# A's blocks 55 steps apart, a block's first scores ahead, and block sums copied by VectorE in a two-attention kernel

## The chip, the cores and the metric

The kernel runs on one core of a Trainium2 chip. The metric is the device time of one execution in microseconds (us); "the time" of a kernel is the median of its timed runs. A profile is one more execution, with its own time.

## The reference, cut to what matters

Two attentions over 2048 positions of width 576 with 32 heads of 18 are computed in fp32, and their outputs stand side by side. A looks, for each position, at 8 positions behind it at distances 0, 2, ..., 14. B looks at all 2048.

```python
def _A_ref(x, wqkv, wo):          # H = 32; Dh = 18; W, dil = 8, 2
    q, k, v = ...                 # x @ wqkv, split into heads
    idx = pos[:, None] - jnp.arange(W) * dil
    logits = jnp.einsum("bhsd,bhswd->bhsw", q, kg) * scale
    logits = jnp.where(idx >= 0, logits, -1e9)
    o = jnp.einsum("bhsw,bhswd->bhsd", _softmax(logits), vg)
    return concat_heads(o) @ wo

def _B_ref(x, wqkv, wo):
    scores = jnp.einsum("bhqd,bhkd->bhqk", q, k) * scale
    o = jnp.einsum("bhqk,bhkd->bhqd", _softmax(scores), v)
    return concat_heads(o) @ wo

return jnp.concatenate([a, b], axis=-1)
```

## The kernel before

Everything is one instruction stream per engine in an order written out by hand (`manual_schedule`). Each engine does its instructions in the order in which the program emits them; so do the queues, of which SP's carries nearly all transfers. An instruction waits where it stands, and everything behind it on its engine or queue waits with it. The waits themselves are put in by the framework: for data, for a buffer that is still read, and for a transfer that has to land.

**Stages.** First come the projections (lines 304 to 717). With them run the first maxima of B. Then comes the main loop (lines 1139 to 1180) of 512 steps, of which step 0 is emitted with the projections. At its end lie B's last output products and `closing`.

**A step.** Step s works on block n = s // 16 of B and on key tile kt = s % 16. A block is one group g = n // 4 of four heads and one stretch b = n % 4 of 512 queries. In a step TensorE forms the scores of four heads (`score`, line 256, matmul at line 263), 128 keys by 512 queries each, into a ring of four PSUM banks. ScalarE takes each exponential out of its bank (line 268). The step's products with the values are emitted one step later by `weigh` (line 728, matmul at line 731) and add up over the block's 16 steps in the bank `po`. There is one `po`. After the last key tile, in the step with kt = 0 of the next block, `finish` (line 736) copies `po` into the tile `o` by ScalarE (line 740) and plans the division and the store over the next 26 steps.

**Maxima.** The exponent of a query needs its row maximum beforehand. Therefore TensorE also forms the scores with queries and keys exchanged (`take`, line 160), and VectorE reduces each bank to its maxima (`reduce`, line 168). These run ahead of the scores by some blocks. A step has three such reductions: `maximum(1)`, the half pieces of both row groups (`parts_of_maximum`, line 233, shared by two steps) and `maximum(0)`. Their matmuls use a ring of three banks. In the order of TensorE a step is: one half piece, score 0, `maximum(1)`, score 2, score 1, the other half piece, score 3, `maximum(0)`, then the eight instructions of line 731. When 64 reductions of a block are there, `least` (line 173) takes the block's negated maximum, `turn` transposes it one step later, `halve` (on GpSimd, lines 103 and 104) splits it one step after that, and `place` (line 191) writes it with eight small SP transfers into rows 54, 55 and 118, 119 of the block's query tile `qs`. From halve to place are 5 steps, or 2 in the last group. A block's first score waits for its eight transfers.

**Agenda.** `plan(start, pieces)` and `later(n, f)` put functions into `agenda[step]`. `due()` runs those of the current step at its end. `inside` holds functions that the next step runs ahead of its last score.

**A.** A's attention is done in 8 blocks of 256 positions by GpSimd, spread over the main loop by `local(j)` (line 845). The pieces of block j stand at fixed distances from its start, which is 10 + 54 j: nine `match` (lines 868 and 872) at distance 5 to 25, VectorE's maxima over the window (`most`, line 886) at 31 to 33, `lower` (line 892) at 33, the exponential at 35, the sums (`total`) at 36 to 38, `share` (line 905) at 39, nine `weighted` (lines 911 to 914) at 39 to 59, `upper` and `rest` at 60 and 61, and two stores to DRAM (`put`) at 64 and 66. `get` loads the result back transposed (six SP transfers, lines 936 and 938) into the tiles `at0`, `at1` and `ahl`, of which there is one each. Two products with the output weights follow for each of the two halves of 128 positions (`sums_of_a`, line 946, matmuls at line 1036), in the steps after those that `MADE` lists. The second half's `get` stands at the step in which the first half's second product runs. So it waits on SP until TensorE has done with the tiles. A product carries two maxima with it while there are any. `producing` is the set of steps that have a product of A or B in them.

**The last group.** `fetch_old(b)` (line 980) loads B's finished head outputs back, eight SP transfers each of 126 rows of 2 KB. They stand at steps 448 + 4, 24, 34 and 36 for b = 0, 1, 3 and 2. `full` and `partial` plan B's output products (`sum_of`, line 1044): VectorE copies one bank (line 1055) and adds the other (line 1056).

Of the kernel before, what the change touches and what calls it, by code (L numbers as in the profile page):

```python
# [10 lines left out]
AF = mybir.ActivationFunctionType  # L11
# [8 lines left out]
DH = 18  # L20
# [19 lines left out]
EARLY_PAIRS = EARLY * NB * PIECES + 2  # L40
AHEAD = 7

GAP = 54

A_FROM = 10

MADE = ((88, 96, 112, 128), (144, 160, 176, 192), (201, 208, 224, 240), (250, 256, 272, 288),
        (304, 320, 336, 352), (361, 368, 384, 400), (412, 416, 432, 448), (466, 468, 475, 480))


def ap(t, *dims):
# [10 lines left out]
def two_attentions(ctx: ExitStack, tc, xa, wa, woa, xb, wb, wob, out):  # L62
# [190 lines left out]
    e_room = None  # L253
    counted = [-1]

    def score(g, b, kt, h, kind="scores"):

        assert (g, b) in placed
        qs, ks = sets[g % 3]
        p, r = divmod(h, 2)  # L260
        ps = bank(kind)
        at = slice(64 * r, 64 * r + 56)
        nc.tensor.matmul(ps, ks[at, p, 128 * kt : 128 * kt + 128], qs[at, b, p], start=True, stop=True)  # L263

        counted[0] += 1
        early = counted[0] % 8 < 6
        e = (e_room if early else work).tile([128, 512], F32, name="e", bufs=6 if early else 2)
        nc.scalar.activation(e, ps, AF.Exp, scale=SCALE)  # L268
        return e
# [466 lines left out]
    def finish(g, b):  # L736
        o = work.tile([128, 512], F32, name="o", bufs=2)
        if g == NG - 1 and b == NB - 1:
            return closing(b, o, work.tile([128, 512], F32, name="rec", bufs=1))
        nc.scalar.activation(o, po, AF.Copy)  # L740
        den = work.tile([128, 16], F32, name="den", bufs=2)
        rec = work.tile([128, 512], F32, name="rec", bufs=1)
        parts = []

        def room():
            if g == NG - 1 and b == 0:

                parts[:] = [ap(work.tile([128, 4, 128], F32R, name=f"at{i}", bufs=1), (1, 512)) for i in range(2)]
            else:
                n = work.tile([128, 2, 512], F32R, name="n", bufs=1)  # L750
                parts[:] = n[:, 0], n[:, 1], n
            return parts

        if g == NG - 1 and b > 0:
            return shortly(b, o, rec, *room()[:2])

        def store():
            if g < NG - 1:
                load(do[:, g, :, 512 * b : 512 * b + 512].rearrange("i p n -> p i n"), parts[2].bitcast(F32))
            else:  # L760
                plan(step, full(b, parts))

        for at, f in ((1, lambda: load(den, o[DH:128:32])),
                      (8, lambda: nc.vector.reciprocal(den, den)),
                      (9, lambda: load(drec[g, b].rearrange("i (p n) -> (i p) n", n=16), den)),
                      (13, lambda: load(rec, rows(drec[g, b], (512, 4), (0, 32), (1, 512)))),
                      (18, lambda: nc.gpsimd.tensor_mul(o, o, rec)),  # L767
                      (19, lambda: nc.gpsimd.tensor_copy(room()[0], o)),
                      (20, lambda: nc.gpsimd.tensor_sub(parts[1], o, parts[0])),
                      (26, store)):  # L770
            later(at, f)
# [47 lines left out]
    wo = {}  # L819

    producing = set()

    def load_wo(k, src, *pieces):

# [20 lines left out]
    def local(j):  # L845
# [20 lines left out]
        def match(c):  # L866
            pr = wide()
            nc.gpsimd.tensor_mul(pr, ap(st["q"][:, 2 * c], (SUB, 2), (0, W), (1, SUB)), window(st["k"], c))  # L868
            if c == 0:
                st["pr"] = pr  # L870
            else:
                nc.gpsimd.tensor_add(st["pr"], st["pr"], pr)  # L872
            if c == DH // 2 - 1:
                lg = st["lg"] = work.tile([128, W, SUB], F32, name="lg", bufs=1)
                nc.gpsimd.tensor_add(lg, st["pr"][:, 0], st["pr"][:, 1])
                if j == 0:
                    for w in range(1, W):
                        nc.gpsimd.memset(lg[:32, w, : DIL * w], MASKED)
# [46 lines left out]
        def put(i):  # L925
            load(rows(dao[j, i, 0, 0], (DH * SUB, 128), (1, DH * SUB)),
                 ap(st["parts"][i].bitcast(F32), (1, DH * SUB)))
# [18 lines left out]
        def sums_of_a(h):  # L946
# [7 lines left out]
            nc.scalar.activation(y, two, AF.Copy)  # L954
            behind_scores.append(lambda: nc.vector.tensor_add(y, one, y))

        pieces = [(33, lower), (35, exponents), (39, share), (60, upper), (61, rest), (64, lambda: put(0)), (66, lambda: put(1))]

        pieces[:0] = [(at, lambda f=f, n=n: f(n)) for f, ats in ((most, (31, 32, 33)), (total, (36, 37, 38)),
                                                                (inverses, (38, 39))) for n, at in enumerate(ats)]  # L960
        for c in range(DH // 2):
            pieces.append((5 + 5 * c // 2, lambda c=c: match(c)))
            pieces.append((39 + 5 * c // 2, lambda c=c: weighted(c)))

        for nm, at, apart in (("q", -18, 2), ("k", -10, 2)) if j else (("q", -9, 1), ("k", -5, 1)):
            pieces += [(at + apart * i, lambda nm=nm, i=i: fetch(nm, i)) for i in range(4)]
        pieces += [(16 + 2 * i, lambda i=i: fetch("v", i)) for i in range(4)]
        made = [p - A_FROM - GAP * j for p in MADE[j]]
        for n, ends in enumerate((made[:2], made[2:])):
            pieces.append((max(ends[0] - 8, made[1] + 1 if n else 0), lambda n=n: get(n)))  # L970
            for h in range(2):
                pieces.append((ends[h], lambda h=h: finished(h)))
                producing.add(A_FROM + GAP * j + ends[h] + 1)
            pieces.append((ends[1] + 6, lambda n=n: load(out[p0 + 128 * n : p0 + 128 * n + 128, :D], ys["a", j, n])))
        return pieces

# [67 lines left out]
    def sum_of(y, t, h, chunks, kind=None):  # L1044

        pos, cols = slice(128 * t, 128 * t + 128), slice(288 * h, 288 * h + 288)
        both = []
        for r in range(2):
            both.append([])
            for c, (hi, lo) in enumerate(chunks):  # L1050
                at = slice(64 * r, min(64 * r + 64, hi.shape[0]))
                whi, wlo = wo["b"][c]
                both[r] += [(a[at, pos], w[at, cols]) for a, w in ((hi, whi), (hi, wlo), (lo, whi))]
        one, two = beside(kind, *both)
        nc.vector.tensor_copy(y, one)
        nc.vector.tensor_add(y, two, y)

    def first(t, b, h):
# [55 lines left out]
    ):  # L1114
        plan(start, [(4 * c, lambda k=k, src=src, ch=ch: load_wo(k, src, *ch)) for c, ch in enumerate(chunks)])
    for j in range(NJ):
        plan(A_FROM + GAP * j, local(j))
    for g in range(1, NG):
        if g > EARLY:
            plan(STEPS * (g - 2) + 1, [(n, f) for n, f in enumerate(stack_loads(g))])  # L1120
        if g == NG - 1:
            plan(STEPS * g, [(4, lambda: fetch_old(0)), (24, lambda: fetch_old(1)), (34, lambda: fetch_old(3)),
                             (36, lambda: fetch_old(2))])
            plan(STEPS * g, [(n, lambda t=t, h=h: partial(t, h)) for n, (t, h) in
                             zip((40, 41, 42, 44, 46, 48), [(t, h) for t in range(3) for h in range(2)])])
            plan(STEPS * g, [(62, lambda: outside.append(lambda: first(3, NB - 1, 0)))])
            for b in range(NB - 1):
                producing.update(STEPS * g + NT * (b + 1) + (31 if b == 0 else 7) + n for n in range(8))
        plan(STEPS * (g - 1), [(24, lambda g=g: load_v(g))])
# [10 lines left out]
    while step < ALL:  # L1140
        n, kt = divmod(step, NT)
        g, b = divmod(n, NB)
        es = [None] * 4

        whole = total - sum(given) > 1
        parts = bool(begun) or total - sum(given) > 3

        ps = bank() if inside and whole else None
        if parts:
            part = parts_of_maximum()  # L1150
        for h in (0, 2, 1, 3):

            if inside and h == 3:
                inside.pop(0)()
            es[h] = score(g, b, kt, h)
            if h == 0 and whole:
                maximum(1, ps)()
            if h == 1 and parts:
                part()
            if h == 3 and whole:  # L1160
                maximum(0)()
        for fs in (behind_scores, outside):
            while fs:
                fs.pop(0)()

        paired = paired or kt % 2 == 0 and sum(given) == total and not begun
        for _ in range(1 if paired and step < ALL - 2 else len(waiting)):
            if waiting:
                waiting.pop(0)()
        if ready and (kt % 2 == 0 or not paired):  # L1170
            weigh(ready.pop(0))
        ready.append((g, b, kt, es))
        if paired and kt % 2:
            weigh(*ready)
            ready.clear()
        due()

        if len(waiting) > (0 if not paired else 2 if kt % 2 else len(waiting)):
            waiting.pop(0)()
        step += 1  # L1180
# [24 lines left out]
```

## Time and profile before

| what | value |
|---|---|
| timed runs | 1616.1, 1617.08, 1619.99 us; median 1617.08 |
| the profiled execution's own time | 1616.82 us |
| its span, first to last instruction | 1615.0 us |
| projections, to the first exponential of the main loop | 413.8 us |
| main loop to step 480 | 1067.8 us |
| steps 480 to 511 | 120.4 us |
| the rest | 13.0 us |

In the page, a group's row gives line, engine, operation, output and inputs with shapes, count, then busy time, mean ns of one, idle time of the engine just before, and what ended it. A row of the timeline gives the start from the span's beginning, the duration, engine, line, operation and count; in square brackets is the idle time of the engine just before it and what ended that. PEld is TensorE's weight load, which runs ahead of and beside PE's matmuls. SPq is the issuing of transfers on SP's queue; a row gives the time of issue and not of landing. A row of the waits gives who waited for whom, the total in us, the count and the longest. The view of windows gives, for each stretch, its length and then each engine's busy time with its count of instructions, the granted TensorE clock as a share, the DMA engines' busy share and GB/s. Since each step ends with the eight matmuls of line 731, their starts are used as marks of the steps.

### The profile page before, as it was taken

What the parts mean: (1) busy time and instruction counts of PE and PEld (TensorE: products, weight loads), DVE (VectorE), ACT (ScalarE), POOL (GpSimd) and SP (SyncE); (2) the same over time, 40 slices, a digit from 0 to 9 for tenths busy, and PEclk for the clock granted to TensorE, in tenths of its full rate; (3) what the DMA queues carried; (4) which work ended last, traced back from release to release, by engine and by line L of the source; (5) the groups of instructions that cost most, each with busy time, mean ns of one, the idle gap of its engine ahead of it and who ended that gap; (6) DMA issues with size and microseconds to landing.
All of it is one profiled execution on the core that took longest, in us unless ns stands there. A gap on an engine that the chain in (4) does not pass through costs nothing.

```text
span 1615.0 us, 35230 instructions
## 1 busy us (share of the span) xinstructions
PE 1599.0 (99%) x13394; PEld 959.5 (59%) x13394; DVE 1393.9 (86%) x2366; ACT 1212.4 (75%) x2419; POOL 961.1 (60%) x792
## 2 busy tenths in 40 slices
PE   9999999999999999999999999999999999999998
PEld 7999888999544444444444444444444444445676
DVE  5199999999899998999999999999999999999532
ACT  6424442121799998999999999999999999998444
POOL 2405742210265995996995995995996997920000
PEclk9999999999999999999999999999999999999999
DMA  8937954432222262254235235332532241034201
GB/s 250 239 121 196 275 164 133 134 104 79 60 56 64 73 147 54 62 118 113 62 85 133 72 98 115 98 91 60 125 106 58 59 135 47 22 124 139 89 38 60
DMA packets 186058, 172.11 MB, mean 107 GB/s; under 512 B 119152, under 2 KB 132976, under 8 KB 184160
## 3 DMA queue, kind: packets, MB, share of 16 engines
q1 hardware_dynamic: 181024, 158.31, 35.3%
q0 software_dynamic: 4032, 10.63, 3.1%
q8 instruction: 105, 1.72, 0.5%
q10 hardware_dynamic: 832, 0.92, 0.2%
q14 instruction: 65, 0.53, 0.1%
HBM read 96.94 MB, written 71.90 MB: 105 GB/s over the span
## 4 chain that ended last, share of the span: by engine, by line
PE 82%; POOL 7%; DVE 5%; DMA 3%; ACT 2%; issue 1%; SPq 0%; POOLq 0%; DVEq 0%; ACTq 0%
PE po L731 24%; PE bank L160 15%; PE bank L353 15%; PE bank L263 15%; PE bank L1036 8%; PE bank L290 5%; DVE mx L168 4%; ACT e L268 2%; POOL pr L868 1%; POOL pr L872 1%; POOL pr L911 1%; DMA akv<-da 1%; DMA dqk<-olo 1%; POOL pr L912 1%; POOL pr L913 0%
## 5 line engine op out<-in xcount | busy, mean ns | idle before, releaser
L168 DVE TENSOR_REDUCE mx<-bank 128x2 f32<-128x512 f32 x2048 | 1286.0, 684 | 114.5 <-PE bank L160 86.2
L268 ACT ACTIVATE e<-bank 128x512 f32<-128x512 f32 x2048 | 1050.2, 607 | 90.3 <-PE bank L263 83.2
L160 PE MATMUL bank<-ks,qs 54*128 54x256 f32 (+1 forms) x2536 | 791.8, 377 | 7.4 <-DVE mx L168 5.9
L160 PEld LDWEIGHTS bank<-ks,qs 54*128 54x128 f32 x2536 | 411.3, 184 | 464.6 <-DVE mx L168 423.4
L263 PE MATMUL bank<-qs,ks 56*128 56x512 f32 x2048 | 567.3, 426 | 0.1
L731 PE MATMUL po<-e,v 128*19 128x512 f32 x4096 | 537.9, 599 | 0.0
L263 PEld LDWEIGHTS bank<-qs,ks 56*128 56x128 f32 x2048 | 299.3, 185 | 14.7 <-issue 7.5
L868 POOL TENSOR_TENSOR pr<-aq,akv 128x1024 f32<-128x1024 f32 x72 | 158.5, 2202 | 15.4 <-DMA akv<-da 12.8
L911 POOL TENSOR_TENSOR pr<-lg,akv 128x1024 f32<-128x1024 f32 x72 | 158.5, 2201 | 0.6
L872 POOL TENSOR_TENSOR pr<-pr 128x1024 f32<-128x1024 f32 x64 | 152.6, 2384 | 5.0
L731 PEld LDWEIGHTS po<-e,v 128*19 128x19 f32 x4096 | 70.5, 97 | 129.4 <-issue 127.0
L681 ACT ACTIVATE ohi<-bank 128x512 f32<-128x512 f32 (+1 forms) x56 | 30.4, 595 | 152.5 <-issue 100.7
L353 PE MATMUL bank<-xhi,ahi 64*128 64x512 f32 (+1 forms) x448 | 113.5, 387 | 0.0
L353 PE MATMUL bank<-xhi,alo 64*128 64x512 f32 (+1 forms) x448 | 112.3, 387 | 0.0
L353 PE MATMUL bank<-xlo,ahi 64*128 64x512 f32 (+1 forms) x448 | 111.9, 388 | 0.1
L912 POOL TENSOR_TENSOR pr<-pr 128x512 f32<-128x512 f32 x72 | 92.5, 1285 | 5.6
L401 POOL TENSOR_TENSOR alo<-raw,ahi 128x512 fp32r<-128x512 f32 (+1 forms) x14 | 17.6, 1258 | 120.7 <-ACT ahi L400 88.8
L493 POOL TENSOR_TENSOR olo<-olo,ohi 128x512 fp32r<-128x512 f32 x36 | 46.2, 1294 | 66.1 <-ACT ohi L492 57.5
L767 POOL TENSOR_TENSOR o<-o,rec 128x512 f32<-128x512 f32 x29 | 37.6, 1297 | 58.7 <-ACT e L268 34.2
L103 POOL CAST mh<-mt 128x32 fp32r<-128x32 f32 x32 | 6.9, 217 | 102.3 <-DVE mt L183 99.5
L353 PEld LDWEIGHTS bank<-xhi,ahi 64*128 64x128 f32 (+1 forms) x448 | 65.0, 181 | 2.9
L353 PEld LDWEIGHTS bank<-xhi,alo 64*128 64x128 f32 (+1 forms) x448 | 63.9, 182 | 2.9
(197 smaller groups left out, 1827.6 us busy)
## 6 DMA issues: line engine op xcount, KB each, us to landing
do<-n SPq DMA_DIRECT2D x28, 512.0 KB
da<-ohi SPq DMA_DIRECT2D x52, 256.0 KB
akv<-da SPq DMA_DIRECT2D x64, 175.5 KB
out<-y SPq DMA_DIRECT2D x32, 288.0 KB
qs<-dqk SPq DMA_DIRECT2D x30, 288.0 KB
ks<-dqk SPq DMA_DIRECT2D x30, 288.0 KB
at<-dao SPq DMA_DIRECT2D x64, 128.0 KB
rec<-drec SPq DMA_DIRECT2D x29, 256.0 KB
```

The source lines that it names most:

```text
L160: return nc.tensor.matmul(ps if part is None else ps[:, 256 * r : 256 * r + 256], qs[at, b, p, 128 * t : 128 * t + 128], ks[at, p, 512 * k ...
L168: nc.vector.tensor_reduce(at, ps.rearrange("q (s n) -> q s n", s=2), axis=AX.X, op=ALU.max)
L263: nc.tensor.matmul(ps, ks[at, p, 128 * kt : 128 * kt + 128], qs[at, b, p], start=True, stop=True)
L268: nc.scalar.activation(e, ps, AF.Exp, scale=SCALE)
L290: nc.tensor.matmul(ps, a, b, start=c == i == 0, stop=c == 4 and i == 1)
L353: nc.tensor.matmul(ps, a, b, start=start, stop=stop)
L731: nc.tensor.matmul(po[32 * i : 32 * i + 19], vs[g][:, kt, 19 * i : 19 * i + 19], es[i], start=kt == 0, stop=kt == NT - 1)
L868: nc.gpsimd.tensor_mul(pr, ap(st["q"][:, 2 * c], (SUB, 2), (0, W), (1, SUB)), window(st["k"], c))
L872: nc.gpsimd.tensor_add(st["pr"], st["pr"], pr)
L911: nc.gpsimd.tensor_mul(at, ap(st["lg"], (0, 2), (SUB, W), (1, SUB)), window(st["v"], c))
L912: nc.gpsimd.tensor_add(at[:, :, :4], at[:, :, :4], at[:, :, 4:])
L1036: nc.tensor.matmul(ps, a, b, start=start, stop=stop)
```

## The change

- A's blocks start at 10, 67, 122, ..., 397 (12 + 55 j) and no longer at 10 + 54 j. The list of steps for A's products is new.
- In block 0 everything from `most` on stands three steps sooner; its `match` pieces stay.
- In the first step of each block (kt = 0) score 0's matmul is issued ahead of the half piece (`score` gets an argument `between`).
- `finish` copies `po` by VectorE where the next step has no product and the maxima are not all given. The next step then leaves out its half piece, so that its reduction comes later.
- `sum_of` copies the first bank by ScalarE where it is called without a kind (the products outside of the steps' scores).
- `fetch_old(1)` stands at 448 + 28 and no longer at 448 + 24, and `fetch_old(2)` at 448 + 38 and no longer at 448 + 36.

```diff
-GAP = 54
-
-A_FROM = 10
-
-MADE = ((88, 96, 112, 128), (144, 160, 176, 192), (201, 208, 224, 240), (250, 256, 272, 288),
-        (304, 320, 336, 352), (361, 368, 384, 400), (412, 416, 432, 448), (466, 468, 475, 480))
+AT = [10] + [12 + 55 * j for j in range(1, S // AB)]
+
+MADE = ((88, 96, 112, 128), (144, 160, 176, 192), (200, 208, 224, 240), (253, 256, 272, 288),
+        (306, 320, 336, 352), (362, 368, 384, 400), (417, 432, 440, 448), (472, 474, 480, 483))
...
-    def score(g, b, kt, h, kind="scores"):
+    def score(g, b, kt, h, kind="scores", between=None):
...
         nc.tensor.matmul(ps, ks[at, p, 128 * kt : 128 * kt + 128], qs[at, b, p], start=True, stop=True)
+        if between:
+            between()
...
-        nc.scalar.activation(o, po, AF.Copy)
+        if step + 1 in producing or sum(given) == total:
+            nc.scalar.activation(o, po, AF.Copy)
+        else:
+
+            nc.vector.tensor_copy(o, po)
+            copied.add(step + 1)
...
+        soon = 0 if j else 3
         pieces = [(33, lower), (35, exponents), (39, share), (60, upper), (61, rest), (64, lambda: put(0)), (66, lambda: put(1))]
...
         for c in range(DH // 2):
-            pieces.append((5 + 5 * c // 2, lambda c=c: match(c)))
             pieces.append((39 + 5 * c // 2, lambda c=c: weighted(c)))
+        pieces = [(at - soon, f) for at, f in pieces]
+        pieces += [(5 + 5 * c // 2, lambda c=c: match(c)) for c in range(DH // 2)]
...
-        made = [p - A_FROM - GAP * j for p in MADE[j]]
+        made = [p - AT[j] for p in MADE[j]]
...
-                producing.add(A_FROM + GAP * j + ends[h] + 1)
+                producing.add(AT[j] + ends[h] + 1)
...
-        nc.vector.tensor_copy(y, one)
+        if kind:
+            nc.vector.tensor_copy(y, one)
+        else:
+            nc.scalar.activation(y, one, AF.Copy)
         nc.vector.tensor_add(y, two, y)
...
-        plan(A_FROM + GAP * j, local(j))
+        plan(AT[j], local(j))
...
-            plan(STEPS * g, [(4, lambda: fetch_old(0)), (24, lambda: fetch_old(1)), (34, lambda: fetch_old(3)),
-                             (36, lambda: fetch_old(2))])
+            plan(STEPS * g, [(4, lambda: fetch_old(0)), (28, lambda: fetch_old(1)), (34, lambda: fetch_old(3)),
+                             (38, lambda: fetch_old(2))])
...
-        parts = bool(begun) or total - sum(given) > 3
+        parts = (bool(begun) or total - sum(given) > 3) and step not in copied
...
-        if parts:
-            part = parts_of_maximum()
+
+        ahead = kt == 0
+        part = [parts_of_maximum()] if parts and not ahead else []
...
-            es[h] = score(g, b, kt, h)
+            es[h] = score(g, b, kt, h, between=(lambda: part.append(parts_of_maximum())) if parts and ahead and h == 0 else None)
...
             if h == 1 and parts:
-                part()
+                part[0]()
```

More of the change, by code (lines that the diff above doesn't have):

```diff
@@ L821, in two_attentions @@
     producing = set()
+    copied = set()
     def load_wo(k, src, *pieces):
```

## The prediction

> **What bounds the kernel now.** I read the page's groups first, then the waits, then the timeline around the first steps of blocks, and last SP's queue near the end. Three ends meet in the main loop:
>
> ```profile
> PE 1599.0 (99%) x13394; PEld 959.5 (59%) x13394; DVE 1393.9 (86%) x2366; ACT 1212.4 (75%) x2419; POOL 961.1 (60%) x792
> ...
> PEld bank L160 <- DVE mx L168: 423.4, 495, 3.8
> ...
> ACT e L268 <- PE bank L160: 5.8, 13, 1.9
> ...
> PEld po L731 <- ACT o L740: 1.8, 6, 0.3
> ```
>
> PE looks full, but nearly once in each step (495 times) its next weight load waits for a reduction of VectorE's to free a bank. So an ordinary step is a ring: half piece, `maximum(1)`, two reductions, next half piece. How long it is, and what the first steps of a block add, stands in the timeline around block 4's first step (step 64):
>
> ```profile
> 546.90 1.06 PE L731 MATMUL po<-e,v 128*19 128x512 f32 x8
> ...
> 548.92 1.05 PE L731 MATMUL po<-e,v 128*19 128x512 f32 x8
> ...
> 549.91 0.18 PEld L160 LDWEIGHTS bank<-ks,qs 54*128 54x128 f32 x1 [0.85 <-DVE mx L168]
> ...
> 550.27 0.18 PEld L263 LDWEIGHTS bank<-qs,ks 56*128 56x128 f32 x1 [0.18 <-issue]
> ...
> 551.28 1.05 PE L731 MATMUL po<-e,v 128*19 128x512 f32 x8
> ...
> 552.37 2.47 DVE L168 TENSOR_REDUCE mx<-bank 128x2 f32<-128x512 f32 x4
> ...
> 552.74 0.63 ACT L740 ACTIVATE o<-po 128x512 f32<-128x512 f32 x1
> ...
> 553.53 1.05 PE L731 MATMUL po<-e,v 128*19 128x512 f32 x8
> ...
> 555.80 1.05 PE L731 MATMUL po<-e,v 128*19 128x512 f32 x8
> ```
>
> From mark to mark an ordinary step takes 2.02 us; I use 2.03. The three steps around the block's start take 2.36, 2.25 and 2.27. The excess is 0.33, 0.22 and 0.24.
>
> **The change, part by part.** *First scores ahead.* The 0.33 is the issue gap ahead of the first score: PE goes through the waits for the eight placed transfers only after the half piece, which itself waited 0.85 us for VectorE. With the score first, these waits fall into the 0.85. ScalarE's 13 waits of this kind hold 1.95 at step 489, outside of first steps, and 0.32 at step 480 (treated below). What is left is 5.8 - 1.95 - 0.32 = 3.5 us over eleven first steps (blocks 1 to 5, 20, 24, 25, 27 to 29). I take -3.5; the bounds are that and 0, should the waits take as long where they then stand.
>
> *Block sums by VectorE.* By the rule in `finish` and the list of products, eight sums move: those finished at steps 16, 32, 48, 64, 80, 304, 416 and 464. In six of them PE waits for ScalarE's copy now (the row with count 6). The copy takes a slot among the exponentials, which gives the excess of 0.22 and 0.24. On VectorE it stands behind the step's third reduction. The nearest rows of that engine are the reduction of the same shape and a smaller copy:
>
> ```profile
> L168 DVE TENSOR_REDUCE mx<-bank 128x2 f32<-128x512 f32 x2048 | 1286.0, 684 | 114.5 <-PE bank L160 86.2
> ...
> L1055 DVE COPY y<-bank 128x288 f32<-128x288 f32 x24 | 10.9, 456 | 49.0 <-PE bank L1036 49.0
> ```
>
> The copy lies between 0.46 (no longer than the small one) and 0.81 us (456 x 512/288); I take 0.68, the row of equal shape. In the timeline above it would start where the fourth reduction does, 0.6 behind 552.37, and end at 553.65. That is 0.12 behind 553.53, and the 0.46 goes: -0.34 each, six times -2.0 (bounds 0 and -2.8). VectorE does no more, since the reduction left out pays for the copy. At blocks 18 and 25 a product hid the copy, and that product now lies elsewhere. There a product costs 2.1 more than an ordinary step (1452.96 to 1457.12 between marks, quoted with SP's queue below) and in a first step it costs about as much with the copy's excess, so +0.3 for both (bounds 0 and 0.9). The eight reductions left out come at the end, in steps with products, where PE is the bound:
>
> ```profile
> 1541.72 0.63 PE L263 MATMUL bank<-qs,ks 56*128 56x512 f32 x4
> 1542.19 0.64 PE L1036 MATMUL bank<-qs,qs 64*128 64x288 f32 x2
> ...
> 1481.66:1602.05 120.39, 119.37 (x1322) 83.79 (x1323) 52.66 (x108) 67.61 (x131) 8.15 (x13) 1.00 0.18 67
> ```
>
> Four matmuls of 512 columns take 0.47, so 8 x 0.12 = +1.0. `sum_of`'s copy by ScalarE: 0 (bounds -0.5 and +1.5). ScalarE has done with its exponentials by then, since it is busy for 67.6 of the last 120.4 us.
>
> *A's spacing.* Once in the main loop VectorE waits for GpSimd's scores of A, at block 1's `most`:
>
> ```profile
> 522.06 1.28 POOL L905 TENSOR_TENSOR lg<-lg,as 128x512 f32<-128x512 f32 x1 [7.07 <-ACT e L268]
> ...
> 621.31 1.26 POOL L875 TENSOR_TENSOR lg<-pr 128x512 f32<-128x512 f32 x1
> ...
> 622.61 0.43 DVE L886 TENSOR_TENSOR am<-lg 128x256 f32<-128x256 f32 x1 [3.38 <-POOL lg L875]
> ...
> 522.06:622.57 100.51, 98.74 (x775) 42.89 (x775) 89.33 (x148) 97.30 (x192) 96.83 (x70) 1.00 0.41 99
> 619.30:631.20 11.90, 9.04 (x64) 5.81 (x62) 6.28 (x12) 5.23 (x10) 3.52 (x3) 0.71 0.15 38
> 660.50:666.64 6.14, 6.14 (x64) 3.81 (x63) 5.52 (x9) 4.92 (x11) 5.89 (x6) 1.00 0.29 63
> ```
>
> GpSimd is busy for 96.8 of the 100.5 us from block 0's `share` on, so its end hangs on that start. With `share` three steps sooner it starts about 6 us sooner, less 2.1 for a weight split that then stands behind it. `most` stands three steps later in the program. Together that is more than 9 us against a wait of 3.38, so the wait goes. Its price is the first two steps of block 6 against those of block 7: 11.9 - 6.14 = -5.8. Of this 2.9 is PE's idle time (11.90 - 9.04). The other 2.9 is the granted clock of 0.71 in that stretch: PE starts again at a lower clock. If GpSimd were still late, this would be 0.
>
> *The last group's queue.* Here I expect a new wait. Maxima come three to a step. By step 470 the new kernel is 12 reductions short (eight left out, and four that the two products moved from 467 and 469 to 473 and 475 carry). So block 30's last reduction falls into step 474 and no longer 470, and `place` goes from 474 to 478. Block 30's first score stays at 480. Ahead of `place` in SP's queue stand the second `get` of A's last block (469 becomes 475, as it waits for the product in that step), `fetch_old(1)` (472 becomes 476) and the load of `rec` (477). The same queue before:
>
> ```profile
> 1456.73 0.91 SPq L936 DMA_DIRECT2D at<-dao  x2
> ...
> 1460.24 6.33 SPq L999 DMA_DIRECT2D ks<-do  x8
> 1466.67 1.41 SPq L765 DMA_DIRECT2D drec<-den  x1
> ...
> 1470.59 4.80 SPq L195 DMA_DIRECT2D qs<-mh  x4
> 1476.39 2.52 SPq L195 DMA_DIRECT2D qs<-mt  x4
> 1478.95 0.57 SPq L766 DMA_DIRECT2D rec<-drec  x1
> ```
>
> ```profile
> 1452.96 1.05 PE L731 MATMUL po<-e,v 128*19 128x512 f32 x8
> 1457.12 1.05 PE L731 MATMUL po<-e,v 128*19 128x512 f32 x8
> ...
> 1479.77 1.05 PE L731 MATMUL po<-e,v 128*19 128x512 f32 x8
> ...
> 1481.13 0.18 PEld L263 LDWEIGHTS bank<-qs,ks 56*128 56x128 f32 x1 [0.19 <-issue]
> ```
>
> `get` starts at 1456.73, 0.39 ahead of the mark of the step with the product. The eight places end 22.2 us later at 1478.91, and the score goes at 1481.13 without a wait on them. A free set of places and the DMA engines just ahead of that score show the rest:
>
> ```profile
> 1519.96 2.34 SPq L195 DMA_DIRECT2D qs<-mh  x4
> 1522.41 2.18 SPq L195 DMA_DIRECT2D qs<-mt  x4
> ...
> 1473.00:1477.00 4.00, 4.00 (x37) 1.73 (x36) 3.52 (x7) 2.69 (x6) 0.00 (x0) 1.00 0.46 176
> 1479.00:1480.00 1.00, 1.00 (x12) 0.59 (x14) 0.83 (x3) 1.00 (x3) 0.00 (x0) 1.00 0.01 2
> ```
>
> Free, the issue takes 4.6 us; behind the 2 MB of `fetch_old` it takes 8.3, with the engines at 176 GB/s until it is through. By 1480 all has landed, so landing takes about 1.3. In the new order three transfers between `fetch_old` and `place` (`drec`, `out`, `do`) stand elsewhere and `rec` comes in. I take 20.8 from `get` to the last issue and 22.1 to the landing. The bounds are 16.4 (3.5 + 6.4 + 0.6 + 4.6 + 1.3, no backlog) and 24.4 (1456.73 to 1481.13).
>
> PE needs them much sooner. From the mark of step 475 there are four ordinary steps (8.1) and 1.0 to the first score, so 0.39 + 8.1 + 1.0 = 9.5 us from `get`. PE stands for 22.1 - 9.5 = 12.6 us (bounds 6.9 and 14.9). Behind that score all of PE waits, and so do ScalarE, VectorE and the PE-bound end: nothing covers it. Then comes the low clock. As at block 6 a product follows in the next step, so +2.9 again. Together +15.5 (bounds 9.8 and 17.8).
>
> The Trainium skill (TensorE: Matmul & The Clock Gate, Part 1) has TensorE at half clock after an idle window of about 3.4 us, and until some 3.4 us of sustained work have passed. The trace differs: the low clock came after 2.9 us of idle time in the stretch, and a mean clock of 0.71 over 11.9 us is 6.9 us at half clock. By the page's window the low clock would cost an estimated 1.7 and the sum would be 1621.4.
>
> **The sum**, against the profiled execution's own 1616.8 (its span is 1615.0, and it lies 0.3 below the median): -3.5 - 2.0 + 0.3 + 1.0 - 5.8 + 15.5 = +5.5, so 1622.3; against the median 1622.6.
>
> **The rivals.** (1) *The places are not late*: 1622.6 - 15.5 = 1607. It decides if the score does not wait for the queue, because `get`'s wait ends sooner or the transfers don't stand in the program's order. For it: the queue has never yet held up a first score. Against it: the margin now is at most 2.2 us, and `get` comes six steps later against a fixed score. (2) *Small transfers pass the big ones*: landing after 16.4, so PE stands for 6.9 and then has the low clock, +9.8: 1617. For it: `place` uses few bytes. Against it: its issue was held back from 4.6 to 8.3 us. The Trainium skill (DMA: Bandwidth & Descriptors, Queues, rings and completion order) says that each DMA engine takes descriptors in ring order, but that completion isn't first in, first out per issuing engine, as a transfer uses up to 16 rings. By that rule this case could happen. (3) *A's products late as well*: from `put` to the product are 8 steps in block 4 now (298 to 306) where the least before was 12. If GpSimd and the two transfers need two steps more, PE stands for another 4 us plus 2.9: 1629.5.
>
> **How the numbers follow.** The forecast has a chance of 0.60, rival 1 has 0.20, rival 2 and rival 3 have 0.10 each. The forecast's own range is 1619 to 1626. A measurement here can tell 0.3% (4.9 us) from no change, that is 1612.2 and 1621.9. Of the forecast's 0.60 some 0.38 lie above and 0.22 within; rival 1 is faster, rival 2 the same, rival 3 slower. So faster 0.20, same 0.32, slower 0.48. The range is 1607 to 1627: it cuts rival 1 in half and leaves rival 3 out.
>
> **What would show it.** At step 480 PE should have an idle time of some 13 us ahead of line 263, ended by a transfer into `qs`, with `ks<-do` ahead of `qs<-mh` in SP's queue and a granted clock near 0.5 behind it. VectorE's wait for `lg` and the issue gaps at first steps should be gone, and `o<-po` on VectorE should appear eight times. The forecast is wrong if PE runs through step 480, if `lg` is still waited for, or if a wait appears ahead of line 1036.

## The result, and the profile after

| | before | after |
|---|---|---|
| median of 5 runs each on one chip, us | 1618.72 (1616.10 to 1619.99) | 1634.24 (1632.58 to 1635.47) |
| ratio of the times | | 1.0098 (95% interval 1.0083 to 1.0112) |
| profiled execution, us | 1616.8 | 1633.4 |
| its span, us | 1615.0 | 1631.6 |

The change makes the kernel about 1% slower, beyond the upper end of what was forecast (1622.6, range 1607 to 1627). A "step" below runs from its first exponential (line 268) to that of the next step. Cut at the steps where something happens, the two spans differ as follows; each number is the difference of two such starts in the trace.

```
                    before     after    difference
up to step 0         413.8     413.9       +0.1
steps   0 to 429     951.15    941.59      -9.6
steps 429 to 432       6.60     15.14      +8.5
steps 432 to 479     107.70    107.06      -0.6
steps 479 to 482       8.56     24.58     +16.0
steps 482 to 511     112.14    114.88      +2.7
behind step 511       15.02     14.44      -0.6
```

Of the -9.6 and the +2.7, 2.1 are the price of one product of A: steps 0 to 429 have one fewer than before, and steps 482 to 511 have one more. The gains are there, then, and two short stretches of three steps each eat them more than twice. The waits of the changed kernel name both (us in all, times, longest):

```profile
PE bank L261 <- DMA qs<-mt: 14.2, 1, 14.2
...
DVE am L892 <- POOL lg L881: 6.3, 1, 6.3
...
PEld bank L158 <- ACTq L241: 6.2, 29, 0.2
...
PEld po L731 <- DVE o L744: 2.0, 8, 0.2
...
PE bank L1045 <- DVE mx L166: 0.9, 1, 0.9
...
ACT e L268 <- PE bank L158: 0.6, 3, 0.2
```

The first row is the forecast stall at step 480. The second is a wait that the forecast had declared gone: `am`, the first part of `most`, waits for GpSimd's `lg`. It does so at step 428 now, in A's block 7, and no longer at block 1. The third is new as well. `o` on VectorE appears eight times, as it should. The fifth row lies at step 490 (0.2 before), and the last is what is left of ScalarE's 13 waits of 5.8 us at first steps.

**The last group's queue**, in the timeline (start, duration, what, and in brackets the idle time and its releaser):

```profile
1469.86 0.91 SPq L942 DMA_DIRECT2D at<-dao  x2
...
1473.48 6.22 SPq L1008 DMA_DIRECT2D ks<-do  x8
1479.75 0.55 SPq L771 DMA_DIRECT2D rec<-drec  x1
1480.41 4.93 SPq L193 DMA_DIRECT2D qs<-mh  x4
1486.17 5.99 SPq L193 DMA_DIRECT2D qs<-mt  x4
...
1493.54 0.76 PE L261 MATMUL bank<-qs,ks 56*128 56x512 f32 x1 [14.23 <-DMA qs<-mt]
```

The order is the forecast one: `get`, `fetch_old(1)`, `rec`, `place`. From `get` to the last issue it is 22.3 us (1469.86 to 1492.16), and the score follows 1.4 later. Block 30's shares had been ready since 1472.04, where GpSimd's last instruction on `mt` ends: only the queue is late. What holds `place` back within it stands in the waits of SP between 1480 and 1493:

```profile
SPq L193 <- DMA ks<-do: 3.7, 5, 0.9
SPq L193 <- DMA rec<-drec: 2.2, 1, 2.2
```

The records of SP's transfers name eight semaphores, which they take in turn (in 993 of 996 cases the same one comes back eight issues later), and an issue first waits until the transfer eight issues ahead has landed. This is a wait of the program's own, beside those for data and buffers. For most of `place` it is for one of the fetch's eight transfers (the seventh transfer of `place` is issued at 1488.90, and the last of the fetch has landed at 1488.88), and for the last of `place` it is for `rec`, landed at 1491.64.

**The wait for `lg`**, on GpSimd and VectorE, after and then before:

```profile
1320.07 0.66 POOL L101 CAST qs<-y 126x576 fp32r<-126x576 f32 x1
...
1326.79 0.67 POOL L101 CAST qs<-y 126x576 fp32r<-126x576 f32 x1
...
1338.76 0.67 POOL L101 CAST qs<-y 126x576 fp32r<-126x576 f32 x1
...
1351.91 0.68 POOL L101 CAST qs<-y 126x576 fp32r<-126x576 f32 x1
1352.67 1.42 POOL L102 TENSOR_TENSOR ks<-y,qs 126x576 fp32r<-126x576 f32 x1
1354.03 0.58 POOL L834 MEMSET y<- 128x576 f32 x1
...
1360.52 1.26 POOL L881 TENSOR_TENSOR lg<-pr 128x512 f32<-128x512 f32 x1
1361.81 0.85 DVE L892 TENSOR_TENSOR am<-lg 128x256 f32<-128x256 f32 x1 [6.32 <-POOL lg L881]
```

```profile
1323.73 0.69 POOL L103 CAST qs<-y 126x576 fp32r<-126x576 f32 x1
...
1335.23 0.66 POOL L103 CAST qs<-y 126x576 fp32r<-126x576 f32 x1
...
1342.59 1.30 POOL L875 TENSOR_TENSOR lg<-pr 128x512 f32<-128x512 f32 x1
...
1344.97 1.31 DVE L886 TENSOR_TENSOR am<-lg 128x256 f32<-128x256 f32 x1
```

`qs<-y` and `ks<-y,qs` split a part of the second weight (`load_wo` "b" uses the room of an old `qs` and `ks`). One split takes 2.1 us (0.68 and 1.42). The five splits come at fixed steps, 407 to 423; the start of A's block 7 moved by nine steps, from 388 to 397. Before, two of them stood between block 7's `match` pieces ahead of `lg`, and `lg` was through 1.1 us ahead of `am` (1342.59 + 1.30 against 1344.97). Now four stand there, and a memset.

The granted clock (third number from the right) around the two stalls, and PE at the place of the old one:

```profile
1361.60:1361.80 0.20, 0.00 (x0) 0.00 (x0) 0.00 (x0) 0.00 (x0) 0.20 (x2) 0.87 0.29 113
...
1368.40:1368.60 0.20, 0.20 (x4) 0.20 (x3) 0.01 (x1) 0.20 (x1) 0.20 (x1) 0.56 0.00 0
...
1481.20:1481.40 0.20, 0.00 (x0) 0.00 (x0) 0.00 (x0) 0.00 (x0) 0.00 (x0) 0.54 0.45 133
...
1498.20:1498.40 0.20, 0.20 (x6) 0.20 (x4) 0.14 (x1) 0.20 (x1) 0.00 (x0) 0.80 0.56 143
...
619.30:631.20 11.90, 11.90 (x109) 6.14 (x107) 11.14 (x22) 10.62 (x22) 2.53 (x3) 1.00 0.37 90
```

The clock is at half from within the first row to within the second, and from within the third to within the fourth; PE resumed at 1363.92 and 1493.54. The last row is the stretch that stood at 9.04 us of PE and a clock of 0.71 before: block 1 makes nothing wait any more.

### The profile page after: what moved, and what is told of

Its sections match the earlier page's. It is cut to its first block, busy times and chain, and to the rows that moved or that the text cites. A ratio compares the mean times of both kernels' runs of the same rounds, so it can differ in the third digit from the quotient of the medians.

```text
span 1631.6 us, 35230 instructions
## 1 busy us (share of the span) xinstructions
PE 1598.9 (98%) x13388; PEld 955.9 (59%) x13388; DVE 1385.2 (85%) x2347; ACT 1219.1 (75%) x2438; POOL 960.6 (59%) x792
## 4 chain that ended last, share of the span: by engine, by line
PE 87%; DMA 4%; DVE 3%; POOL 2%; ACT 2%; issue 1%; SPq 1%; POOLq 0%; DVEq 0%; ACTq 0%
PE po L731 28%; PE bank L261 17%; PE bank L158 16%; PE bank L353 14%; PE bank L1045 7%; PE bank L290 5%; DVE mx L166 2%; DMA rec<-drec 2%; ACT e L268 2%; POOL xlo L401 1%; DMA raw<-xa 1%; DMA drec<-den 1%; POOL pr L878 0%; DMA dqk<-olo 0%; SPq L1008 0%
## 5 line engine op out<-in xcount | busy, mean ns | idle before, releaser
L261 PE MATMUL bank<-qs,ks 56*128 56x512 f32 x2048 | 572.0, 428 | 14.2 <-DMA qs<-mt 14.2
L261 PEld LDWEIGHTS bank<-qs,ks 56*128 56x128 f32 x2048 | 301.3, 185 | 61.2 <-ACT e L268 39.3
L353 PEld LDWEIGHTS bank<-xlo,ahi 64*128 64x128 f32 (+1 forms) x448 | 63.9, 182 | 3.5 <-POOL xlo L401 0.5
```

What stands on the lines that cost most here:

```text
L353: nc.tensor.matmul(ps, a, b, start=start, stop=stop)
```

## The experiments

Ratios are to runs of the kernel before beside each (medians 1616.82 to 1617.53 us). All stage times are from the runs' own profiles, cut as in the table above.

**The fetch back at 472.** The changed kernel, with one number undone:

```diff
-            plan(STEPS * g, [(4, lambda: fetch_old(0)), (28, lambda: fetch_old(1)), (34, lambda: fetch_old(3)),
+            plan(STEPS * g, [(4, lambda: fetch_old(0)), (24, lambda: fetch_old(1)), (34, lambda: fetch_old(3)),
```

> The changed kernel with fetch_old(1) of the last groups back at position 24 (step 472), ahead of block 30's second get (475) in SP's queue. Theory (the late place): in the changed kernel PE stands 14.2 us at step 480 because SP issues fetch_old(1), and waits there for room in the queue, ahead of block 30's place. With the fetch out of that way the place is issued some 10 us after the get, against 9.5 us until step 480, so the stall falls to 0 to 2 us, and with the low clock behind it 14 to 16 us go: 1618 to 1620 us. The 6.3 us wait for lg at step 428 stays. Rival (block 30's maxima or its share come too late by themselves, 55 steps apart): the stall at 480 stays above 10 us and the time within 3 us of 1634.

Measured: 1619.93 us (10 runs), 1.0012 of the kernel before (1.0003 to 1.0021). Steps 479 to 482 fall from 24.58 to 11.49. SP's queue and PE, in this kernel's timeline:

```profile
1446.57 6.53 SPq L1008 DMA_DIRECT2D ks<-do  x8
...
1469.96 0.91 SPq L942 DMA_DIRECT2D at<-dao  x2
...
1474.27 0.57 SPq L771 DMA_DIRECT2D rec<-drec  x1
1474.94 2.27 SPq L193 DMA_DIRECT2D qs<-mh  x4
1477.31 2.33 SPq L193 DMA_DIRECT2D qs<-mt  x4
...
1481.01 0.47 PE L261 MATMUL bank<-qs,ks 56*128 56x512 f32 x1 [1.59 <-DMA qs<-mt]
```

With the fetch 23 us ahead of `get` the place is issued in 4.7 us, close to the free price of 4.6, and its last issue ends 9.7 us behind `get`. The 1.59 that are left are `get` and `rec` themselves. The late place is the cause of the stall, and the fetch's position decides it. What the expectation calls room in the queue is the semaphore of the transfer eight issues ahead. What is left of the stretch, 2.9 us (11.49 against 8.56 before), is the price of the later `get` and `place`, the low clock behind the wait included. Block 7's wait is unchanged (steps 429 to 432: 16.04).

**The second weight later.** The changed kernel, with loads and splits of the second weight 16 steps later:

```diff
-        ("b", wob, STEPS * (NG - 2) + 20,
+        ("b", wob, STEPS * (NG - 2) + 36,
```

> The changed kernel with the second weight's loads and splits begun 16 steps later (splits at 423 to 439 rather than 407 to 423). Theory (splits on GpSimd ahead of lg): VectorE's 6.3 us wait for GpSimd's lg at step 428 comes from four splits of about 2.1 us and a memset that stand ahead of block 7's lg in GpSimd's order, where two stood before the change. With them behind lg the wait goes, and with its low clock 8 to 9 us: 1625 to 1627 us. The stall at step 480 stays at 14 us. Rival (55 steps between the blocks leave GpSimd's ordinary o, n, n sets too late by themselves): the wait at 428 stays above 3 us, and the time above 1630. A second way to miss: the later splits delay another wait, which then appears between steps 430 and 460.

Measured: 1627.42 us (4 runs), 1.0056 (1.0041 to 1.0072). Steps 429 to 432 fall from 15.14 to 6.74 (before: 6.60), and steps 432 to 479 stay at 107.05, so that no other wait came up there. The medians differ by 6.8 and not 8.4; this profile lost 3.0 in other places, of them 1.2 in steps 0 to 429. In its timeline `lg` stands ahead of the splits:

```profile
1353.88 1.28 POOL L881 TENSOR_TENSOR lg<-pr 128x512 f32<-128x512 f32 x1
1355.10 0.67 POOL L101 CAST qs<-y 126x576 fp32r<-126x576 f32 x1
...
1357.26 0.90 DVE L892 TENSOR_TENSOR am<-lg 128x256 f32<-128x256 f32 x1
```

The spacing by itself doesn't make block 7 late.

**A smaller dose.** The same edit with 24 in place of 36, 4 steps later.

> The changed kernel with the second weight's loads and splits begun 4 steps later (splits at 411 to 427 rather than 407 to 423), a smaller dose of the 16 steps. Theory (each split ahead of lg costs its own 2.1 us): three splits instead of four stand ahead of block 7's lg on GpSimd, and VectorE's wait at step 428 is 2.1 us shorter, 4.2 us. Rival (the wait comes from the weight's loads on the queues, or from another order): the wait stays at 6.3 us, or goes as a whole.

Measured (one run): three splits start ahead of `lg`, at 1325.95, 1337.91 and 1351.06, and the wait is shorter by 2.4 us; steps 429 to 432 take 13.27.

```profile
1359.13 1.26 POOL L881 TENSOR_TENSOR lg<-pr 128x512 f32<-128x512 f32 x1
...
1360.43 0.85 DVE L892 TENSOR_TENSOR am<-lg 128x256 f32<-128x256 f32 x1 [3.87 <-POOL lg L881]
```

One split fewer is worth about one split (2.1). Together with the run before, this shows that it is their number ahead of `lg`. The time, 1634.15, shows nothing of it, as the run lost as much elsewhere (0.5 up to step 0, 0.8 at step 154, 0.9 at step 480).

**Both.**

> The changed kernel with both edits: the fetch back at 472, and the second weight's splits 16 steps later. Theory: the two stalls are independent, and both go: 1634 less 15 less 9 = 1610 us, within 1608 to 1612, under the kernel before. Rival (one stall covers the other, so that the gains do not add): above 1616 us.

Measured: 1611.64 us (5 runs), 0.9965 (0.9952 to 0.9977), faster than the kernel before. Steps 429 to 432 take 6.68, steps 479 to 482 take 9.36. The two stalls are independent. What is left at step 480 is the row "PE bank L261 <- DMA qs<-mt: 1.0, 1, 1.0" of its waits.

**Without the first scores ahead.** The changed kernel with `ahead = False`.

> The changed kernel without a block's first scores ahead (they are issued where the kernel before has them). Theory (the edit is worth little): the block starts at which PE waits on semaphores go back from about 2.15 to 2.39 us, the others from about 2.16 to 2.05 us, and the sum over 31 starts stays within 1 us of the changed kernel. Rival (the 3.5 us forecast are won, and lost again elsewhere): the block starts together become 3 us or more longer, 1637 us or more.

Measured (one run): 1632.65 us. The 29 steps that end at the first score of blocks 1 to 29 take 64.19 us in all before, 62.91 after and 63.80 here. So the edit is worth 0.9 against this run, 1.3 against the kernel before. It splits in two: at 13 blocks (1 to 5, 17, 24 to 30) the step is 0.1 to 0.3 us shorter with the score ahead, and at most others it is about 0.11 longer. Why longer stands in the timeline of the changed kernel at block 11's start, where PE has no waits for places:

```profile
792.38 1.05 PE L731 MATMUL po<-e,v 128*19 128x512 f32 x8
793.36 0.18 PEld L261 LDWEIGHTS bank<-qs,ks 56*128 56x128 f32 x1 [0.85 <-ACT e L268]
...
794.00 0.18 PEld L158 LDWEIGHTS bank<-ks,qs 54*128 54x128 f32 x1 [0.22 <-ACTq L241]
...
794.53 1.05 PE L731 MATMUL po<-e,v 128*19 128x512 f32 x8
```

The half piece has two matmuls into one bank, and line 241 is the ScalarE no-op that lets the second go once the first is done. With a score of 512 columns in front the first is done later, the no-op too, and the second part's weight load waits 0.22: 2.15 from mark to mark instead of 2.03 to 2.05. The waits count this 29 times (6.2 us in all); in this run, without the score in front, the row is not there. PE's 0.85 are not saved either; another row names their end.

**First scores ahead where they help.** The kernel with both stalls mended, and

```diff
-        ahead = kt == 0
+        ahead = kt == 0 and n in (1, 2, 3, 4, 5, 17, 24, 25, 26, 27, 28, 29, 30)
```

> The kernel with both stalls mended (fetch at 472, second weight's splits 16 steps later), and a block's first scores ahead only at the 13 blocks where their absence cost 0.1 to 0.3 us (1 to 5, 17, 24 to 30). Theory (the order helps where PE's queue holds semaphore waits ahead of the scores, and costs where it doesn't): the other 18 block starts lose 0.11 us less each, 1.9 us in all: 1609.7 against 1611.6 us. Rival (the 0.11 us come back a step later, or the start of a block shifts other work): no difference, within 0.5 us.

Measured: 1610.82 us (5 runs), 0.9956 (0.9942 to 0.9970). Steps 0 to 429 take 940.52 and not 942.26: -1.7. The profile's span is longer all the same, since its part up to step 0, which no edit touches, came out 2.7 longer (415.4 and 412.7), and step 480 0.6. The medians, 1611.64 and 1610.82, don't tell the two kernels apart. At block 11 the stretch that was 2.15 is 2.05 in its timeline:

```profile
793.65 1.05 PE L731 MATMUL po<-e,v 128*19 128x512 f32 x8
794.64 0.18 PEld L158 LDWEIGHTS bank<-ks,qs 54*128 54x128 f32 x1 [0.85 <-DVE mx L166]
...
795.70 1.06 PE L731 MATMUL po<-e,v 128*19 128x512 f32 x8
```

**Block sums by ScalarE again.** The kernel with both stalls mended, and `if True:` ahead of ScalarE's copy in `finish`.

> The kernel with both stalls mended, with all block sums copied out by ScalarE as the kernel before has them. Theory: the eight block starts at which VectorE copies (1 to 5, 19, 26, 29) get 0.34 to 0.41 us longer where no product stands beside them, and the profile's span is 2.5 to 3.0 us longer than with VectorE's copies. Rival (the copy only moves the wait, its gain is that of the maxima left out beside it): the three steps of the start together stay as they are, span within 1 us.

Measured (one run): 1609.82 us, span 1608.0 against 1607.5. Both forecasts missed. Each of the eight block starts does lose 0.41 (0.37 - 0.12 + 0.16 in the three steps), 3.3 in all. But up to step 480 the loss is only 1.1 (1060.30 and 1059.20 us from step 0), as many other steps between are a little shorter, and steps 480 to 511 are 1.6 shorter (119.49 and 121.05), all of it in steps 487 to 490 (21.14 and 22.71). There PE no longer waits 0.9 us for a reduction at step 490 (the fifth row of the waits above). The left-out half pieces run at the end, as the reductions show (least, middle and longest duration in ns, first and last start), with VectorE's copies and then with ScalarE's:

```profile
L166 DVE TENSOR_REDUCE mx<-bank x2048: 620/681/694, 82.3 to 1509.7; 128x2 f32<-128x512 f32 x187
```

```profile
L166 DVE TENSOR_REDUCE mx<-bank x2048: 625/683/699, 82.6 to 1504.8; 128x2 f32<-128x512 f32 x187
```

From step 0 to 511 VectorE's copies cost 0.5 us and don't win 2.5; of one profile each, that is nothing that a time of this kernel can tell.

**A's last products a step sooner.** The kernel of the selective order, with the last entry of `MADE` at (471, 473, 480, 483).

> The kernel of the selective order (both stalls mended, first scores ahead at 13 blocks), and the last group's first two products of A at steps 471 and 473 rather than 472 and 474, so that the second get stands a step sooner in SP's queue. Theory: the 0.8 to 1.1 us that PE still waits at step 480 for the last piece of the place (behind rec's landing) go: 0.8 us less than the kernel of the selective order. Rival (the product's own input lands too late a step sooner): a new wait at 471, up to 2 us longer.

Measured: 1607.99 us (5 runs), 0.9947 (0.9934 to 0.9959), the fastest of the kernels here together with the last one below. The wait for the place is gone from its waits, and steps 479 to 482 take 8.64 and not 9.96. That is 1.3 of the 2.8 us between the medians (0.8 were forecast); the rest is not explained.

**The same with ScalarE's block sums.**

> The kernel with both stalls mended, first scores ahead at 13 blocks and A's last products a step sooner, with all block sums copied out by ScalarE again. Theory (VectorE's copies only put off eight pieces of the maxima, which run at the end instead): with ScalarE's copies the blocks up to step 480 take 1.1 us more and the stretch 480 to 496 takes 1.6 us less, so 0.5 us less in all, 1607.5 against 1608.0 us. Rival (the copies' gain of 0.41 us at each of eight block starts is kept): 2.5 to 3 us longer, 1610.5 to 1611 us.

Measured: 1609.71 us (6 runs), 0.9957 (0.9945 to 0.9970). The forecast of -0.5 is not confirmed, and the two intervals overlap. In this profile steps 0 to 429 take 946.47 and not 940.72, of which 4.2 lie in steps 154 to 156, A's block 2:

```profile
727.30 0.59 SPq L771 DMA_DIRECT2D rec<-drec  x1
...
741.67 1.28 POOL L772 TENSOR_TENSOR o<-o,rec 128x512 f32<-128x512 f32 x1 [5.35 <-ACT e L268]
...
748.96 0.80 DVE L892 TENSOR_TENSOR am<-lg 128x256 f32<-128x256 f32 x1 [1.97 <-POOL lg L881]
```

Here GpSimd stands 5.35 us ahead of `o * rec`, with block 2's last `match` behind it. The row names an exponential, but the semaphore wait in front of the instruction ends with the load of `rec`, at 741.51, which had been issued 14.2 us earlier. Leaving this wait out, the comparison agrees with that of the run before it without VectorE's copies: 1.4 more up to step 480, 1.5 less behind it.

**Block 2 a step later.** The kernel with A's last products a step sooner, and

```diff
-        soon = 0 if j else 3
+        soon = {0: 3, 2: -1}.get(j, 0)
```

> The kernel with both stalls mended, first scores ahead at 13 blocks and A's last products a step sooner, and block 2's chain (most, total and what follows, not the matches) one step later, from step 154 rather than 153. Theory (block 2's most has no room: in the profiles of eleven kernels VectorE finds lg between 1 us early and 2 us late at step 154, and the step and its two followers take 6.5 to 11.3 us): the wait cannot come up, steps 154 to 157 lose 0.5 us and more, the median falls by 0.5 to 1 us to 1607.0 to 1607.5, and the runs lie closer together. Rival (the waits at 154 belong to single profiles): median within 0.3 us of 1608.0, the same spread.

(Ten profiles have this `most` at step 154, those of the changed kernel and of the nine experiments above.) Measured: 1608.15 us (6 runs, 1607.36 to 1610.43), 0.9948 (0.9935 to 0.9961). Block 2's `am` starts without a wait in its profile, and steps 144 to 160 take 0.6 less, but neither the median nor the spread moves. The profile shows why the gain need not be seen: block 3's `am`, which had 1.2 us to spare, waits now, and step 209 takes 5.24 and not 4.05.

```profile
867.14 0.42 DVE L892 TENSOR_TENSOR am<-lg 128x256 f32<-128x256 f32 x1 [1.10 <-POOL lg L881]
```

GpSimd works without a break from block 2's last pieces to block 3's `lg` in both profiles, so that what starts later there ends later: `lg` comes 1.7 us later, counted from step 0. In this profile the wait has moved on by one block.

## Why the prediction was right about the queue and wrong about the time

**The last group's queue: right.** Forecast +15.5, measured +16.0 in steps 479 to 482; `get` to the last issue 20.8 forecast, 22.3 measured. The split was less good, and two errors nearly cancel: 14.2 of idle time (forecast 12.6) and 1.8 besides it, which the forecast put down to the low clock (2.9). The experiment with the fetch back shows the fetch as the cause. Rivals 1 and 2 fell; the last small transfers could not pass the big ones, since they were not issued before these had landed. The step that costed the low clock took its price from block 6, where the clock was at half for another 6.4 us after PE had resumed (623.68 to 630.09 in the trace of before); here it was 4.7. The estimate worked out from the Trainium skill (TensorE: Matmul & The Clock Gate, Part 1), 1.7, comes near the 1.8, but with 4.7 us at half clock and not 3.4, so that this is in part luck.

**A's spacing: the failed step.** That GpSimd's "end hangs on that start", "so the wait goes", was right for block 1, where `lg` now ends 6.8 us ahead of `am`, and the -5.8 came out (-2.83 and -2.97 in steps 96 and 97). But "Once in the main loop VectorE waits for GpSimd's scores of A" was read as the only place that mattered. The spacing moves block j by j + 2 steps from block 1 on, and what GpSimd does at fixed steps doesn't move with it. At block 7, nine steps later, two more splits came to lie ahead of `lg`, where the trace of before shows room for half of one (1.1 us). It costs 8.4 us, by the changed kernel against the one with the weights later (-6.7, -1.6 and -0.1 in steps 429 to 431). This was in none of the forecast's terms nor in the three rivals. It is the largest part of the miss: the range ends at 1627, and with the weights later the kernel was measured at 1627.4.

**First scores ahead: mis-sized.** Forecast -3.5 with bounds of -3.5 and 0, measured -0.9 to -1.3. Eleven of the waits were costed as if each vanished (0.32), and the steps without a wait as if nothing changed there. ScalarE's waits did nearly vanish, from 5.8 to 0.6. But the runs show only 0.22 gained on average at the 13 starts and 0.11 lost at some sixteen others, by the no-op between the half piece's two matmuls. With the score ahead both kinds of start take much the same, mostly 2.12 to 2.18, as if the no-op's delay is paid at each.

**Block sums: right in the step, wrong in the sum.** At a start -0.41 against the forecast -0.34 in six places and, without a product in the way, in the other two as well. The eight reductions at the end cost 1.6 by the run with ScalarE's copies (forecast 1.0, without the wait of 0.9 at step 490), and 2.2 more are lost in the steps between, which the forecast had not. They lie in many single steps of 0.1 to 0.3 us; that the left-out pieces shift the pieces behind them is a guess and not shown. Net, the part is worth nothing; the forecast had -1.0.

**The sum.** The spans differ by 16.6. The queue has 16.0 of it, block 7 has 8.4 and the first scores -1.3; everything else together is -6.5. For that the forecast's terms add up to -2.0 + 0.3 + 1.0 - 5.8 = -6.5 as well. So 11.1 us were missed: 8.4 by a wait not looked for, 2.2 by the first scores and 0.5 by the queue. That the rest meets is in part luck, as the block sums came to nothing. Two parts of the change were not tried alone: `sum_of`'s copy by ScalarE (forecast 0) and the shift of `fetch_old(2)`. Steps 482 to 511 take 0.6 more than the moved product explains, though the late reductions cost 1.6 there, so about 1.0 was won by something that no run here separates.

**What would show it.** Of the signs named, the idle time at step 480, its releaser, the order in the queue and the clock of 0.5 came. "Wrong if `lg` is still waited for" came too. So did, in small, a wait ahead of the products' line (1036 before, 1045 now): 0.9 us at step 490, for a reduction. Rival 3, products late behind block 4, has no sign: no wait stands ahead of line 1045 in steps 300 to 320.

## What to carry to other kernels

When a chain is shifted against a fixed schedule, look at each place where the two meet, not at the one that waits now: the margin of every consumer in the trace of before (`lg`'s end to `am`'s start, eight times) was there to be read, and block 7's 1.1 us could not take two splits of 2.1. A big transfer put ahead of a small urgent one costs more than its own issue, 6.2 us here: most of the small ones also waited for the landing of the transfer eight issues ahead, 5.9 us in all. Taking back a shift of four steps was worth 14 us. And an order that hides one wait may delay a signal that something else hangs on, so it is priced at the places without the wait as well.

## What was not expected of the hardware

**The clock changes on a grid.** From the four rows with fractions above, the changed kernel's half clock lasts from 1361.75 to 1368.58 and from 1481.22 to 1498.28 (in a stretch of 0.20 us, a mean of 0.87 is 0.05 at half). That is 6.83 and 17.06 us, 2 and 5 times 3.41; and from the first to the third edge it is 119.47, 35 times 3.41. The kernel with the fetch back shows a third length:

```profile
1482.20:1482.40 0.20, 0.20 (x5) 0.09 (x8) 0.20 (x2) 0.20 (x2) 0.00 (x0) 0.92 0.17 61
...
1485.60:1485.80 0.20, 0.20 (x6) 0.20 (x6) 0.20 (x1) 0.20 (x2) 0.00 (x0) 0.55 0.34 92
```

1482.37 to 1485.78 is 3.41, once. The Trainium skill (TensorE: Matmul & The Clock Gate, Part 1) has a free-running window of 3413 ns, and the trace agrees. It also has the clock fall after a whole idle window; here 1.59 us without a matmul were enough (the fall came 1.4 us after PE had resumed), while the 1.0 us at the same step in the kernel with both edits brought no fall in a mean clock of 1.00. Nor did 1.60 us in the kernel of the selective order:

```profile
1472.89 0.46 PE L261 MATMUL bank<-qs,ks 56*128 56x512 f32 x1 [1.60 <-DMA qs<-mt]
...
1472.00:1480.00 8.00, 7.11 (x69) 4.52 (x69) 6.08 (x11) 5.26 (x11) 0.40 (x1) 1.00 0.45 155
1608.60:1608.80 0.20, 0.00 (x0) 0.00 (x0) 0.00 (x0) 0.00 (x0) 0.00 (x0) 0.74 0.00 0
```

The same idle time fell differently on the grid. In the first kernel all 1.59 (1479.42 to 1481.01) lie in the 3.41 ahead of the fall at 1482.37. In the second the edge at 1608.70, counted back by 40 times 3.413, gives one at 1472.18, which cuts the idle time (1471.30 to 1472.89) into 0.88 and 0.71. So these two profiles say that what a stall costs in clock depends on where in this grid it falls; no experiment here sets that place on purpose.

**The part ahead of the first step varies.** Of kernels that do the same there, the profiles have 412.7 to 415.4 us up to step 0. These 2.7 us are more than several of the edits are worth; the stage times tell such edits apart where the medians don't.
